# Two linear-attention and two segment-memory layers: one copy of 1024 columns per tile, opening stacks at once, and the last segment's output in column halves

## The chip, the cores and the metric

The kernel runs on one core of one Trainium2 chip. The metric is the device time of one execution in microseconds, as the median of several runs. Engines: PE multiplies matrices (PEld loads its weights), DVE, ACT and POOL work on vectors, and SP issues nearly all DMAs.

## The reference

A sequence of 2048 rows of 512 goes through four layers, each with layer normalisation ahead and a residual sum behind: A, B, A, B. Both have 32 heads of 16.

```python
def A(x):                                  # linear attention
    q, k, v = heads(x @ wqkv)
    pq, pk = q @ w_phi, k @ w_phi          # per head, 16 x 16
    phi_q = concat(softmax(pq), softmax(-pq)); phi_k = concat(softmax(pk), softmax(-pk))
    kv, z = phi_k.T @ v, phi_k.sum(rows)
    return (phi_q @ kv / (phi_q @ z)) @ wo

def B(x):                                  # 4 segments of 512 rows, with a memory M, z
    for s in range(4):
        p = softmax(causal(q[s] @ k[s].T / 4))
        a_mem = phi(q[s]) @ M / (phi(q[s]) @ z)
        o[s] = g * a_mem + (1 - g) * (p @ v[s])
        M, z = M + phi(k[s]).T @ v[s], z + phi(k[s]).sum(rows)
    return o @ wo
```

## The kernel before

Everything is in float32, products in pairs of high and low parts (`hh` and `hl`, `oh` and `ol`, `w` twice), so that one product is three matmuls per 128 rows of the contraction.

**Layer A** has two passes. The first makes keys, values and the sum kv, and stores the projected queries. The second, `pass2`, goes over 16 tiles of 128 rows. Per tile PE turns the tile before (`turn`, four transposes of `tmp` into one bank `g`), multiplies the tile's features with KN (32 small matmuls, which DVE weighs into `tmp`), turns the features of the tile to come (`transposed`, eight transposes into the PSUM tile `lg`, of two banks), and multiplies the output of the tile before with wo (`out_proj`, twelve matmuls). In the first tiles `transposed` stands behind `out_proj`, so the KN product of the same features follows it closely. ACT copies the turned features from PSUM to SBUF (`P`); POOL makes differences and scales them (`scale_q`); DVE sums the exponentials (`es`, `rr`).

**Layer B** is one loop over steps k, in `steps`. Four heads are a group m, five steps each (R = 5), eight groups to a segment, 32 groups in all. In each step `attend` makes scores into `lg`, ACT takes their exponential and POOL masks; `maxima` does the same scores into `mx`, `my` or `g` nine steps ahead (LEAD), for DVE to take their maxima. At the first step of a group PE also multiplies the probabilities of the group before with the values (`weighted`) and turns the result before that (`finish`). The tables FIRST, GAPS, and FINAL or LAST say what else each step does: `2.1 Q3/6` is six steps of the fourth projection in step 1 of group 2. Q, V, O and P are work for PE between the score steps: projections of queries and keys, values, the output of the segment before (`out`, `out_pair`), and the early part of the last output (`early`). LAST ends the first B layer, FINAL the second. `mm3_pair` lets two products of half the rows run side by side in the array; SP hands over between them.

**Stacks.** Scores need queries and keys as three stacked parts. `stack` issues three DMAs of them (`e<-ta`) on SP, for queries (side 0) and for keys (side 1), in steps 2 and 4 of a group (STACK), three groups ahead. The first two groups are stacked before step 0, in the opening, where second pass and layer B run into one another; there q0, v0, k0, v1, q1, k1 and v2 are projected first (BEFORE), and `queue_w` orders the next weights (`wqk`) behind each. SP takes its DMAs in order; one that waits holds those behind it.

Of the kernel before, what the change touches and what calls it, by code (L numbers as in the profile page):

```python
# [15 lines left out]
D = 512  # L16
# [67 lines left out]
"""  # L84
FINAL = """
0.0 a1 a1 max fin  | 0.1 Q2/6          | 0.2 Q2/6          | 0.3 Q2/6 | 0.4 Q2/6
1.0 max fin
2.0 turn max fin   | 2.1 Q3/6          | 2.2 Q3/6          | 2.3 Q3/6 | 2.4 Q3/6
3.0 turn a2 max fin | 3.1 O/6          | 3.2 O/6           | 3.3 O/6 | 3.4 O/6
4.0 turn a2 fin max  # L90
5.0 turn a3 a3 max fin  | 5.1 O/6           | 5.2 O/6           | 5.3 O/6 | 5.4 O/6
6.0 max fin        | 6.4 pre
7.0 pt pt fin max  | 7.1 P/4           | 7.2 P/5           | 7.3 P/5 | 7.4 P/4
"""
BEFORE = {-25: "q0 load", -23: "v0", -21: "k0",
          -18: "n", -17: "v1 n", -16: "n", -15: "n n", -14: "q1 n", -13: "n", -12: "k1 n", -11: "n", -10: "v2 n",
# [4 lines left out]
def interleave_kernel(ctx, tc, x_in, a_wqkv, a_wphi, a_wo, b_wq, b_wk, b_wv, b_wo, b_beta,  # L101
# [396 lines left out]
        wait(end)  # L498
        yield

    def out_pair(tiles, xdst, w):

        pos = [PS("g", G) for _ in tiles]

        def side(po, o):
            return po, lambda a, kc: o[a][:, kc * P : (kc + 1) * P], lambda b, kc: w[b][:, kc, :]

        yield from mm3_pair(*[side(po, o) for po, (x, i, o) in zip(pos, tiles)])

        def end():  # L510
            for po, (x, i, o) in zip(pos, tiles):
                y = T2("tb3", TB3)
                act.copy(y, po)
                pool.tensor_tensor(out=x, in0=y, in1=x, op=ADD)
                sync.dma_start(out=xdst[i], in_=x)
        wait(end)
        yield

    def weigh(out, p, eps, add, eng=pool):
# [123 lines left out]
    class LayerA:  # L643
# [268 lines left out]
        def pass2(self):  # L912

            KN = self.KN
            phT = {}

            def transposed(i):

                if i >= NT:
                    return
                ef = self.e.pop(i).rearrange("p h s f -> p (h s f)")
                phT[i] = T2("P4", NP4, shape=(P, 8, P))
                pt = PS("lg", 1, (P, 2, 512))
                for half in range(2):
                    for q in range(4):
                        g = 4 * half + q
                        tp(pt[:, half, q * P : (q + 1) * P], ef[:, g * P : (g + 1) * P], ident)
                    act.copy(phT[i][:, 4 * half : 4 * half + 4, :], pt[:, half].rearrange("p (g t) -> p g t", g=4))  # L930
                    yield

            yield from transposed(0)
            o = None
            for i in range(NT + 1):
                if i > 0:
                    oT = turn([o[:, c * P : (c + 1) * P] for c in range(NC)])
                    yield PAUSE if i == NT else None
                if i + 2 < NT:
                    exp(self.e[i + 2])  # L940
                if i < NT:
                    o = T2("tmp", 2)
                    f = phT.pop(i)
                    for half in range(2):
                        pn = PS("g", G)
                        pv = pn[:, 0 : 16 * VW].rearrange("p (g h e) -> p g h e", g=4, h=4)
                        for q in range(4):
                            g = 4 * half + q
                            for a in (0, 64):
                                mm(pn[a : a + 64, q * 4 * VW : (q + 1) * 4 * VW], lhsT=f[:, g, a : a + 64],  # L950
                                   rhs=KN[:, g].rearrange("p h e -> p (h e)"), start=True, stop=True,
                                   tile_position=(0, a))
                        weigh(o[:, half * 256 : half * 256 + 256].rearrange("p (g h d) -> p g h d", g=4, h=4),
                              pv, 0.0, False)
                        yield
                    if not 0 < i < 3:
                        yield from transposed(i + 1)
                    if i == 0:
                        self.begun(3)
                    if i + 3 < NT:  # L960
                        self.e[i + 3] = differences(*self.raw.pop(i + 3))
                    if i != 1 and i + 2 < NT:
                        scale_q(self.e[i + 2])
                    self.load_q(i + 4)
                    ahead = residual(self.xsrc, i, ("ot", OT))
                if i > 0:
                    yield from out_proj(x, self.xdst, i - 1, oT, self.wo)
                if 0 < i < 3:
                    yield from transposed(i + 1)
                if i == 1:  # L970
                    scale_q(self.e[i + 2])
                x = ahead


    class LayerB:
        def __init__(self, xsrc, xdst):
            self.xsrc, self.xdst = xsrc, xdst
            self.st, self.hT, self.vv, self.ot, self.mx, self.U = {}, {}, {}, {}, {}, {}
            self.pr, self.at, self.k, self.wo = {}, {}, BEGIN, []
            self.later, self.late, self.rows, self.turned = [], [], [], []  # L980

        def start(self):
# [262 lines left out]
        def out(self, s):  # L1245
            for t in (0, 2):
                tiles = [(x, 4 * s + t + n, oT) for n, (oT, x) in enumerate(self.turned[0:2])]
                del self.turned[0:2]
                yield from out_pair(tiles, self.xdst, self.wo)

        def early(self):

# [6 lines left out]
            for t in (0, 2):  # L1259
                o, po = [], []  # L1260
                for n in range(2):
                    o.append(turn([b[:, t + n] for b in ot]))
                    yield
                po = [PS("g", G) for _ in range(2)]

                def side(po, o):
                    return po, lambda a, kc: o[a][:, kc * P : (kc + 1) * P], lambda b, kc: self.wo[b][:, kc, :]

                if t == 0:
                    yield from mm3_pair(side(po[0], o[0]), side(po[1], o[1]), range(NC - 1))  # L1270
                else:
                    for n in range(2):
                        yield from mm3(*side(po[n], o[n]), range(NC - 1))

                def end(po=po, xs=self.xe[t : t + 2]):
                    for p, x in zip(po, xs):
                        dve.tensor_tensor(out=x, in0=p, in1=x, op=ADD)
                wait(end)
                yield
# [31 lines left out]
        def steps(self, side, after, table_end):  # L1311
# [81 lines left out]
            for k in range(BEGIN, R * N + 1):  # L1393
# [9 lines left out]
                for f in self.at.pop(k, []):  # L1403
                    f()
                m = k // R + 3
                if k % R in STACK and 0 <= m < N:
                    self.stack(m, STACK.index(k % R))
                if k == R * N:
                    for _ in range(4):
                        next(early)  # L1410
                if k % R == 0 and 0 <= k // R - 1 < N:
                    self.weighted(k // R - 1)
                for f in self.rows:
# [43 lines left out]
    run(p1[0], prepare())  # L1457
    for i in range(2):
        lb = LayerB(xs[2 * i + 1], xs[2 * i + 2])
        run(p1[i])  # L1460
        a2 = la[i].pass2()
        opening = lb.opening()
# [39 lines left out]
```

## Time and profile before

| | us |
|---|---|
| median of 3 runs (1478.45 to 1483.07) | 1481.69 |
| profiled execution | 1485.13 |
| its span, first to last instruction | 1483.4 |
| PE busy | 1385.0 |
| DVE busy | 1059.2 |
| ACT busy | 814.4 |
| POOL busy | 692.8 |
| mean granted PE clock | 0.986 |

Busy times overlap; they do not add up. A wait counts only where the waiting engine has nothing else and the end depends on it. In the timeline a row is start, duration, engine, line, operation, output and input, and in brackets the idle time before it and what ended it. The second passes lie at about 190 to 325 and 904 to 1046 us, the openings of layer B at 262 to 295 and 980 to 1010, and the last segment from 1366 to the end.

### The profile page before, as it was taken

Reading aid. Unit: us, or ns where it says so; the run is one execution under the profiler, and the core shown is the slowest. Engines: PE = TensorE matmul, PEld = TensorE weight load, DVE = VectorE, ACT = ScalarE, POOL = GpSimd, SP = SyncE. Lnnn points to the kernel's source line nnn. Section 1 sums busy time; section 2 is a strip of 40 time slices with the busy share of each in tenths; the row PEclk is TensorE's granted clock in tenths of the full one; section 3 lists DMA queues with packets and bytes.
Section 4 is the critical chain, followed back from the end, with each engine's and each line's share of the span. In section 5 each row is a group of like instructions: output and inputs, shape, how many; then the busy total and the mean of one; then the engine's idle time right before and its main releaser. Section 6 shows DMA issues by size and latency. Waiting matters only on the chain.

```text
span 1483.4 us, 33426 instructions
## 1 busy us (share of the span) xinstructions
PE 1385.0 (93%) x12412; PEld 1048.7 (71%) x12412; DVE 1059.2 (71%) x3258; ACT 814.4 (55%) x1226; POOL 692.8 (47%) x1024
## 2 busy tenths in 40 slices
PE   7999988899999999999999998898998999999887
PEld 6887867666676776777578887776666777777554
DVE  4666777477787787888656677746678878778772
ACT  5545345336566677576634434442556756766653
POOL 1568655304446547335324365532335556643341
PEclk9999999999999999999999999999999999999898
DMA  5387355435444444445431006643453453543431
GB/s 188 115 305 270 129 162 166 131 101 148 143 129 119 126 130 130 126 130 162 137 128 57 23 23 196 203 144 95 128 178 95 134 149 92 137 126 91 103 88 54
DMA packets 108786, 196.05 MB, mean 132 GB/s; under 512 B 14416, under 2 KB 27856, under 8 KB 107856
## 3 DMA queue, kind: packets, MB, share of 16 engines
q1 hardware_dynamic: 107472, 193.38, 43.8%
q8 instruction: 99, 1.62, 0.5%
q10 hardware_dynamic: 1152, 0.52, 0.1%
q14 instruction: 63, 0.52, 0.1%
HBM read 101.05 MB, written 39.85 MB: 95 GB/s over the span
## 4 chain that ended last, share of the span: by engine, by line
PE 71%; DVE 11%; ACT 7%; POOL 4%; issue 3%; DMA 3%; SPq 1%; ACTq 0%; DVEq 0%; POOLq 0%
PE g L178 53%; PE lg L178 6%; PE g L182 5%; ACT P L156 4%; PE mx L178 3%; PE lg L182 2%; PE my L178 1%; DVE es L156 1%; POOL P L156 1%; DVE g L156 1%; POOL tb L156 1%; SPq L156 1%; ACT U L156 1%; DVE my L156 1%; DVE mx L156 1%
## 5 line engine op out<-in xcount | busy, mean ns | idle before, releaser
L156 ACT ACTIVATE P<-lg 128x1024 f32<-128x1024 f32 x320 | 329.4, 1029 | 183.5 <-PE lg L178 103.1
L156 POOL TENSOR_SCALAR_AFFINE_SELECT P<-P 128x256 f32<-128x256 f32 (+1 forms) x448 | 193.6, 447 | 333.4 <-ACT P L156 333.1
L156 DVE CUSTOM_DVE_ANT_0 mx<-mx,mask 128x128 f32<-128x128 f32 (+3 forms) x332 | 165.1, 497 | 55.2 <-PE my L178 45.2
L156 DVE CUSTOM_DVE_ANT_0 g<-g,mask 128x512 f32<-128x512 f32 x360 | 175.8, 543 | 18.7 <-PE g L178 17.9
L178 PE MATMUL g<-hh,wqk 64*128 64x512 f32 (+1 forms) x960 | 184.9, 392 | 3.7 <-SPq L156 1.5
L178 PE MATMUL lg<-e,e 64*128 64x256 f32 (+2 forms) x1024 | 156.1, 359 | 23.1 <-ACT P L156 23.0
L178 PE MATMUL g<-w,oh 64*128 64x512 f32 (+1 forms) x728 | 169.4, 406 | 7.5 <-SPq L156 6.1
L156 DVE CUSTOM_DVE_ANT_0 my<-my,mask 128x128 f32<-128x128 f32 (+3 forms) x332 | 172.2, 519 | 0.0
L178 PE MATMUL g<-P,v 128*32 128x512 f32 (+3 forms) x2048 | 156.1, 446 | 4.6 <-DVE mxs L156 4.3
L178 PEld LDWEIGHTS lg<-e,e 64*128 64x128 f32 x1024 | 93.8, 189 | 74.2 <-ACT P L156 50.0
L178 PE MATMUL g<-w,hh 64*128 64x512 f32 (+2 forms) x800 | 145.4, 357 | 0.6 <-DVE ol L156 0.6
L156 DVE DVE_READ_ACCUMULATOR2_ANT mxs<- 128x1 f32 x1024 | 143.7, 140 | 0.0
L178 PEld LDWEIGHTS g<-P,v 128*32 128x32 f32 x2048 | 61.0, 112 | 93.3 <-issue 67.7
L156 POOL TENSOR_SCALAR tb<-tb 128x512 f32<-128x512 f32 x72 | 110.9, 1552 | 27.2 <-ACT tb L156 27.2
L178 PEld LDWEIGHTS g<-hh,wqk 64*128 64x128 f32 (+1 forms) x960 | 104.2, 185 | 20.6 <-SPq L156 2.0
L178 PEld LDWEIGHTS g<-w,oh 64*128 64x128 f32 (+1 forms) x728 | 93.7, 190 | 28.2 <-SPq L156 8.7
L178 PE MATMUL g<-hl,wqk 64*128 64x512 f32 (+1 forms) x480 | 106.1, 390 | 0.5 <-DVE hl L156 0.5
L156 ACT COPY tb<-g 128x512 f32<-128x512 f32 x144 | 80.4, 588 | 46.7 <-PE g L178 44.8
L178 PE MATMUL g<-w,ol 64*128 64x512 f32 (+1 forms) x364 | 104.0, 400 | 0.4 <-DVE ol L156 0.4
L178 PEld LDWEIGHTS g<-w,hh 64*128 64x128 f32 (+1 forms) x800 | 92.0, 187 | 13.4 <-DVE ol L156 1.0
L178 PE MATMUL mx<-e,e 63*128 63x256 f32 (+2 forms) x332 | 89.7, 334 | 7.6 <-DMA e<-ta 7.6
L156 DVE TENSOR_TENSOR ol<-g,oh 128x512 fp32r<-128x512 f32 (+1 forms) x66 | 43.6, 673 | 74.5 <-ACT oh L156 74.5
(148 smaller groups left out, 2983.1 us busy)
## 6 DMA issues: line engine op xcount, KB each, us to landing
e<-ta SPq DMA_DIRECT2D x384, 128.0 KB
wqk<-wqk SPq DMA_DIRECT2D x64, 512.0 KB
x<-x SPq DMA_DIRECT2D x48, 256.0 KB
ot<-in SPq DMA_DIRECT2D x28, 256.0 KB
pq<-tb SPq DMA_DIRECT2D x24, 256.0 KB
tb<-pq SPq DMA_DIRECT2D x24, 256.0 KB
x<-xr SPq DMA_DIRECT2D x22, 256.0 KB
xr<-x SPq DMA_DIRECT2D x20, 256.0 KB
```

The lines of the kernel that those rows point to most:

```text
L156: i = f(*a, **k)
L178: return held(nc.tensor.matmul(*a, **k))
L182: return held(nc.tensor.transpose(*a))
```

## The change

It has three parts.

1. `transposed` copies the two halves of `lg` in one instruction of 1024 columns, behind the eighth transpose.
2. The first two groups are stacked, queries and keys, at the first slot of their group of steps (steps -15 and -10).
3. In FINAL the work is dealt anew. Of the last segment's groups 0 to 7, group 1 gets the projection Q3 that stood in group 2; the output of the segment before, which stood in groups 3 and 5, goes in halves of 256 columns over groups 2 to 5 (`thin`); the early output's first half goes from group 7 to 6 and its second half from the end to group 7. Turning two tiles at a time (`turn turn`) and the memory reads (`a2 a2`, `a3 a3`) move accordingly. In `early` the second half is now done by `mm3_pair` too, in both B layers.

```diff
-2.0 turn max fin   | 2.1 Q3/6          | 2.2 Q3/6          | 2.3 Q3/6 | 2.4 Q3/6
...
-4.0 turn a2 fin max
...
+1.0 turn turn max fin | 1.1 Q3/6       | 1.2 Q3/6          | 1.3 Q3/6 | 1.4 Q3/6
...
+4.0 turn turn fin max | 4.1 O/6        | 4.2 O/6           | 4.3 O/6 | 4.4 O/6
...
-    def out_pair(tiles, xdst, w):
+    def out_pair(tiles, xdst, w, w0=0, w1=D):
...
-            return po, lambda a, kc: o[a][:, kc * P : (kc + 1) * P], lambda b, kc: w[b][:, kc, :]
+            return (po[:, 0 : w1 - w0], lambda a, kc: o[a][:, kc * P : (kc + 1) * P],
+                    lambda b, kc: w[b][:, kc, w0:w1])
...
+        for po, (x, i, o) in zip(pos, tiles):
+            y = T2("tb3", TB3)[:, 0 : w1 - w0]
+            act.copy(y, po[:, 0 : w1 - w0])
+            pool.tensor_tensor(out=x[:, w0:w1], in0=y, in1=x[:, w0:w1], op=ADD)
+            if w1 == D:
                 sync.dma_start(out=xdst[i], in_=x)
...
-                    act.copy(phT[i][:, 4 * half : 4 * half + 4, :], pt[:, half].rearrange("p (g t) -> p g t", g=4))
+                    if half == 1:
+                        act.copy(phT[i].rearrange("p g t -> p (g t)"), pt.rearrange("p h x -> p (h x)"))
...
-                yield from out_pair(tiles, self.xdst, self.wo)
+                parts = 2 if self.thin and s == NSEG - 2 else 1
+                for n in range(parts):
+                    yield from out_pair(tiles, self.xdst, self.wo, n * D // parts, (n + 1) * D // parts)
...
-                if t == 0:
-                    yield from mm3_pair(side(po[0], o[0]), side(po[1], o[1]), range(NC - 1))
-                else:
-                    for n in range(2):
-                        yield from mm3(*side(po[n], o[n]), range(NC - 1))
+                yield from mm3_pair(side(po[0], o[0]), side(po[1], o[1]), range(NC - 1))
...
-                if k % R in STACK and 0 <= m < N:
-                    self.stack(m, STACK.index(k % R))
+                if 0 <= m < N:
+                    for side_ in range(2):
+                        if k % R == (STACK[side_] if m > 1 else 0):
+                            self.stack(m, side_)
                 if k == R * N:
                     for _ in range(4):
-                        next(early)
+                        next(early, None)
```

On ACT, in the second pass (P is the SBUF copy or the features, lg the PSUM tile, oh the high part of the turned output), before:

```order
L156 CAST oh_2346<-g_2348 128x512
L156 ACTIVATE P_388_2316<-P_388_2316 128x1024
L156 COPY P_402_2381<-lg_2382 128x512 x2
L156 CAST oh_2421<-g_2423 128x512
L156 ACTIVATE P_404_2393<-P_404_2393 128x1024
```

and after:

```order
L156 CAST oh_2341<-g_2343 128x512
L156 ACTIVATE P_388_2311<-P_388_2311 128x1024
L156 COPY P_402_2376<-lg_2377 128x1024
L156 CAST oh_2415<-g_2417 128x512
L156 ACTIVATE P_404_2387<-P_404_2387 128x1024
```

Two copies have become one; nothing changes place.

On SP, in the first opening (e is a stack, ta the high or low part of a projection, wqk weights, x the second pass's output on its way to memory), before:

```order
L156 DMA wqk_3071<-wqk_82 128x1024
L156 DMA wqk_3126<-wqk_81 128x1024
L156 DMA e_432_2495<-ta_544_3026 32x2x512 x2
L156 DMA e_432_2495<-ta_545_3027 32x2x512
L156 DMA wqk_3157<-wqk_82 128x1024
L156 DMA e_433_2496<-ta_556_3073 32x2x512
L156 DMA e_433_2496<-ta_557_3074 32x2x512
L156 DMA e_433_2496<-ta_556_3073 32x2x512
L156 DMA x_10_93<-ot_2906 128x512
```

and after:

```order
L156 DMA wqk_3058<-wqk_82 128x1024
L156 DMA e_432_2488<-ta_544_3013 32x2x512 x2
L156 DMA e_432_2488<-ta_545_3014 32x2x512
L156 DMA e_433_2489<-ta_556_3060 32x2x512
L156 DMA e_433_2489<-ta_557_3061 32x2x512
L156 DMA e_433_2489<-ta_556_3060 32x2x512
L156 DMA wqk_3119<-wqk_81 128x1024
L156 DMA wqk_3147<-wqk_82 128x1024
L156 DMA e_432_2488<-ta_544_3013 32x2x512 x2
```

The first group's six stack DMAs now stand ahead of the two weight loads, and the second group's right behind these.

On PE, in steps 1 and 2 of group 4 of the last segment (lg: scores, mx, my and the `g` of e and e: scores for the maxima), before:

```order
L178 MATMUL lg_18969<-e_2273_12060,e_2274_12061 128x512 x2
L178 MATMUL mx_18976<-e_2293_12143,e_2292_12142 128x256
L178 MATMUL my_18977<-e_2293_12143,e_2292_12142 128x256
L178 MATMUL mx_18976<-e_2293_12143,e_2292_12142 128x384
L178 MATMUL my_18977<-e_2293_12143,e_2292_12142 128x384
L178 MATMUL lg_18986<-e_2273_12060,e_2274_12061 128x256 x2
L178 MATMUL lg_18986<-e_2273_12060,e_2274_12061 128x384 x2
```

and after, from the last maxima of step 1 on:

```order
L178 MATMUL my_19034<-e_2293_12139,e_2292_12138 128x384
L178 MATMUL g_19043<-w_13651,oh_18989 128x256
L178 MATMUL g_19044<-w_13651,oh_19000 128x256
L178 MATMUL g_19043<-w_13652,oh_18989 128x256
L178 MATMUL g_19044<-w_13652,oh_19000 128x256
L178 MATMUL g_19043<-w_13651,ol_18990 128x256
L178 MATMUL g_19044<-w_13651,ol_19001 128x256
L178 MATMUL g_19043<-w_13651,oh_18989 128x256
L178 MATMUL g_19044<-w_13651,oh_19000 128x256
L178 MATMUL g_19043<-w_13652,oh_18989 128x256
L178 MATMUL g_19044<-w_13652,oh_19000 128x256
L178 MATMUL g_19043<-w_13651,ol_18990 128x256
```

Before, the scores of a step follow the maxima of the step before at once; now six pairs of the output, 256 columns wide, lie between them.

More of the change, by code (lines that the diff above doesn't have):

```diff
@@ L86 @@
 0.0 a1 a1 max fin  | 0.1 Q2/6          | 0.2 Q2/6          | 0.3 Q2/6 | 0.4 Q2/6
-1.0 max fin
-2.0 turn max fin   | 2.1 Q3/6          | 2.2 Q3/6          | 2.3 Q3/6 | 2.4 Q3/6
-3.0 turn a2 max fin | 3.1 O/6          | 3.2 O/6           | 3.3 O/6 | 3.4 O/6
-4.0 turn a2 fin max
-5.0 turn a3 a3 max fin  | 5.1 O/6           | 5.2 O/6           | 5.3 O/6 | 5.4 O/6
-6.0 max fin        | 6.4 pre
-7.0 pt pt fin max  | 7.1 P/4           | 7.2 P/5           | 7.3 P/5 | 7.4 P/4
+1.0 turn turn max fin | 1.1 Q3/6       | 1.2 Q3/6          | 1.3 Q3/6 | 1.4 Q3/6
+2.0 max fin        | 2.1 O/6           | 2.2 O/6           | 2.3 O/6 | 2.4 O/6
+3.0 a2 a2 max fin  | 3.1 O/6           | 3.2 O/6           | 3.3 O/6 | 3.4 O/6
+4.0 turn turn fin max | 4.1 O/6        | 4.2 O/6           | 4.3 O/6 | 4.4 O/6
+5.0 a3 a3 max fin  | 5.1 O/6           | 5.2 O/6           | 5.3 O/6 | 5.4 O/6
+6.0 max fin pre    | 6.1 pt pt         | 6.2 P/6           | 6.3 P/6 | 6.4 P/6
+7.0 pt pt max fin  | 7.1 P/4           | 7.2 P/5           | 7.3 P/5 | 7.4 P/4
 """
@@ L499, in out_proj @@
         yield
-    def out_pair(tiles, xdst, w):
+    def out_pair(tiles, xdst, w, w0=0, w1=D):
         pos = [PS("g", G) for _ in tiles]
         def side(po, o):
-            return po, lambda a, kc: o[a][:, kc * P : (kc + 1) * P], lambda b, kc: w[b][:, kc, :]
+            return (po[:, 0 : w1 - w0], lambda a, kc: o[a][:, kc * P : (kc + 1) * P],
+                    lambda b, kc: w[b][:, kc, w0:w1])
         yield from mm3_pair(*[side(po, o) for po, (x, i, o) in zip(pos, tiles)])
[L510 to L514, printed above, removed]
+        for po, (x, i, o) in zip(pos, tiles):
[3 more added lines that the diff above has]
+            if w1 == D:
                 sync.dma_start(out=xdst[i], in_=x)
-        wait(end)
         yield
@@ L978, in __init__ @@
             self.st, self.hT, self.vv, self.ot, self.mx, self.U = {}, {}, {}, {}, {}, {}
-            self.pr, self.at, self.k, self.wo = {}, {}, BEGIN, []
+            self.pr, self.at, self.k, self.wo, self.thin = {}, {}, BEGIN, [], False
             self.later, self.late, self.rows, self.turned = [], [], [], []
@@ L1459, in interleave_kernel @@
         lb = LayerB(xs[2 * i + 1], xs[2 * i + 2])
+        lb.thin = i == 1
         run(p1[i])
```

## Prediction

> **What bounds the kernel.** I read the page first, for the engine that the end hangs on, then the waits of that engine, then the timeline at each place the change touches, then one row per block of the last segment.
>
> ```profile
> PE 1385.0 (93%) x12412; PEld 1048.7 (71%) x12412; DVE 1059.2 (71%) x3258; ACT 814.4 (55%) x1226; POOL 692.8 (47%) x1024
> PE 71%; DVE 11%; ACT 7%; POOL 4%; issue 3%; DMA 3%; SPq 1%; ACTq 0%; DVEq 0%; POOLq 0%
> ...
> PE lg L182 <- ACT P L156: 23.3, 32, 1.1
> PE lg L178 <- ACT P L156: 23.0, 53, 1.3
> ...
> PE mx L178 <- DMA e<-ta: 7.6, 2, 4.2
> ```
>
> PE is busy 93% of the span and 71% of the chain that ended last, so a saving must be a saving of PE time. The three waits (total us, times, longest) belong to the three parts of the change: 32 waits of the transposes of the second linear pass (16 tiles, two passes) on the copy; the waits of score matmuls on the exponential, most of all where no projection lies between them, as in parts of the last segment; and two waits on the opening stacks, one in each B layer.
>
> **Part 1, one copy of 1024 columns.** PE in one tile of the second pass, and POOL and DVE beside it:
>
> ```profile
> 940.97 0.60 PE L182 MATMUL g<-ident,tmp 128*128 128x128 f32 x4
> 942.60 0.66 PE L182 MATMUL lg<-ident,P 128*128 128x128 f32 x4
> 943.93 0.66 PE L182 MATMUL lg<-ident,P 128*128 128x128 f32 x4 [0.68 <-ACT P L156]
> 944.34 0.71 PE L178 MATMUL g<-w,oh 128*128 128x512 f32 x2
> ...
> 946.84 1.06 POOL L156 TENSOR_TENSOR P<-P,rr 128x512 f32<-128x512 f32 x1 [1.86 <-DVE rr L156]
> 947.21 0.60 PE L182 MATMUL g<-ident,tmp 128*128 128x128 f32 x4
> 948.83 0.66 PE L182 MATMUL lg<-ident,P 128*128 128x128 f32 x4
> ```
>
> The second four transposes start 1.33 us after the first four and wait for the copy of the first half. Four take 0.41 (943.93 to 944.34). In the batch the second four follow at once: 1.33 - 0.41 = 0.92 us of PE time less. Nothing else in the tile makes PE wait, so a tile falls from 6.24 us (940.97 to 947.21) to about 5.3. The copy loses its overlap and is read later, but the matmuls that read it stand in the next tile, more than 4 us on.
>
> That holds for tiles 4 to 15. In tiles 0 to 3 the matmuls with KN follow the transposes at once:
>
> ```profile
> 920.45 0.60 PE L182 MATMUL lg<-ident,P 128*128 128x128 f32 x4
> ...
> 922.80 1.17 PE L178 MATMUL g<-KN,P 128*64 128x68 f32 x32
> ...
> L156 ACT ACTIVATE P<-lg 128x1024 f32<-128x1024 f32 x320 | 329.4, 1029 | 183.5 <-PE lg L178 103.1
> ```
>
> Today 2.35 us lie between them. The new copy is not in the trace; its bounds are nothing above one old copy (0.59 us, the second in the old order) and two of them (1.18). The nearest row is the exponential of the same PSUM tile and size, 1.03. Transposes 0.41 + 0.66, copy 1.03, some 0.1 of semaphores: 2.2. So these eight tiles gain 0.1 each or lose as much, and I take 0. Part 1: 24 x 0.92 = 22.1.
>
> What is late next: POOL's multiplication of the following tile ends at 947.90 and its transposes start at 948.83, 0.93 later. With tiles 0.92 shorter that slack is gone in the tiles where DVE also does layer statistics, as here. I take off 0.5 us per pass (bounds 0 and the whole 0.92 in half of the tiles, 5.5).
>
> A rule against this part stands in the Trainium skill, PSUM — Partial Sum Buffer, Summary: rules for kernel authors: to read PSUM while matmuls run, aim at a different bank. The two halves are two banks of 512 FP32 each, so by it halves could overlap and the batch would give the overlap away. The trace disagrees for this program: the second half waited all the same (0.68 us, above). By that rule alone part 1 would be worth 0 and not 22.
>
> **Part 2, opening stacks.** PE, then DVE and SP's queue before it, then PE in the first layer, and the stretch behind each stall (columns: length, PE, PEld, DVE, ACT, POOL, clock, DMA share, GB/s):
>
> ```profile
> 1003.54 0.55 PE L178 MATMUL mx<-e,e 63*128 63x256 f32 x1 [3.42 <-DMA e<-ta]
> 1004.37 1.22 PE L178 MATMUL g<-w,oh 128*128 128x512 f32 x2
> ...
> 990.55 0.69 DVE L156 TENSOR_TENSOR ta<-tb,ta 128x512 fp32r<-128x512 f32 x1 [4.75 <-ACT ta L156]
> 989.27 5.76 SPq L156 DMA_DIRECT2D wqk<-wqk  x2
> 995.13 1.86 SPq L156 DMA_DIRECT2D e<-ta  x3
> 997.86 2.05 SPq L156 DMA_DIRECT2D e<-ta  x3
> ...
> 285.61 0.35 PE L178 MATMUL mx<-e,e 63*128 63x256 f32 x1 [4.18 <-DMA e<-ta]
> ...
> 286.00:289.00 3.00, 3.00 (x9) 2.10 (x8) 1.64 (x8) 0.00 (x0) 3.00 (x3) 0.50 0.00 0
> 1003.50:1009.00 5.50, 5.46 (x30) 4.14 (x30) 2.52 (x10) 0.81 (x2) 4.29 (x4) 0.50 0.02 8
> ```
>
> The last part that a stack copies is ready at 991.24 (DVE), but its DMAs stand behind the second of two weight loads, which waits for PE till about 994.7 (995.03 less its own issue); the stack is issued by 999.91 and lands at 1003.5, 3.6 us later. Moved ahead of that load, six DMAs of about 0.6 us start at 989.6, wait for 991.24, and end by about 993.5; with the same 3.6 they land at 997.1. PE gets there at about 1000.1 (1003.54 less its wait). The stall goes whole: 3.4 + 4.2 = 7.6. The two loads behind wait for PE as they do now, and the second stack's six DMAs follow them with the time of a whole head group. Stores to x, now behind these, are awaited by nobody here.
>
> After the stall the granted clock is 0.50. In 5.5 us, half of the PE time is the excess: 2.7; in the first layer 3.0 us: 1.5. Both go with the stall. Part 2: 7.6 + 4.2 = 11.8. In the 40 us behind it DVE is the busiest after PE, and without stall and half clock it is nearly full; I take off 1 us a layer (bounds 0 and 2).
>
> **Part 3, the last segment.** One row for each of the head groups 1 to 6 (score step to score step, columns as above), and last a group of the second segment, where halves of 256 columns already fill every step:
>
> ```profile
> 1378.54:1393.06 14.52, 11.28 (x75) 5.75 (x74) 9.95 (x38) 7.99 (x11) 5.13 (x9) 0.65 0.36 94
> 1393.06:1405.26 12.20, 12.20 (x126) 9.21 (x126) 9.06 (x36) 7.58 (x11) 3.68 (x8) 1.00 0.37 88
> 1405.26:1417.89 12.63, 12.34 (x126) 9.36 (x126) 11.86 (x42) 8.81 (x12) 8.39 (x11) 1.00 0.38 101
> 1417.89:1432.88 14.99, 10.76 (x83) 5.99 (x82) 10.52 (x42) 6.82 (x9) 3.67 (x8) 0.77 0.35 92
> 1432.88:1445.00 12.12, 11.52 (x119) 8.38 (x118) 9.09 (x38) 6.95 (x9) 6.16 (x10) 1.00 0.07 26
> 1445.00:1458.83 13.83, 9.12 (x59) 4.35 (x58) 0.92 (x3) 6.44 (x8) 3.71 (x8) 0.63 0.27 95
> ...
> 1087.07:1098.74 11.67, 9.86 (x118) 6.83 (x117) 8.01 (x33) 6.77 (x10) 3.82 (x9) 1.00 0.56 159
> ```
>
> Groups 1, 4 and 6 have no projection between the score steps. They are the longest: PE waits for the exponential, and its clock falls to 0.63 to 0.77. The change fills all of them. Splitting columns adds no PE time: three pairs of 256 take 0.35, half of three pairs of 512.
>
> ```profile
> 1075.22 0.40 PE L178 MATMUL g<-w,hh 64*128 64x256 f32 x4
> 1075.46 0.28 PE L178 MATMUL g<-w,hl 64*128 64x256 f32 x2
> ...
> 1405.90 0.64 PE L178 MATMUL g<-w,oh 64*128 64x512 f32 x4
> 1406.37 0.41 PE L178 MATMUL g<-w,ol 64*128 64x512 f32 x2
> ```
>
> (Two pairs, then the third: 0.24 and 0.47 to the third.) New: group 0 gets eight transposes behind it (0.82, partly in PE's wait for U), +0.5; 1 has the projection, 12.1; 2 to 5 half filled, 11.67 as the row of the second segment, to which turning or memory reads add 0.1 to 0.4 that partly lie in PE's wait for U: 11.8, 11.9, 11.8, 11.6; 6 has the last output's first half and no maxima, 11.5. Sum 71.2, against 80.3 now: 9.1. Bounds: 12.6 for every half-filled group (the fullest row at full clock), 5.7 in all; 11.4 for each, 10.5.
>
> At the end PE now turns and multiplies the last output's second half: six matmuls ahead of the last values, twelve behind them while DVE weighs:
>
> ```profile
> 1465.44 0.44 PE L182 MATMUL g<-ident,ot 128*128 128x128 f32 x2
> ...
> 1468.48 2.36 PE L178 MATMUL g<-P,v 128*32 128x512 f32 x32
> 1471.65 0.66 PE L182 MATMUL g<-ident,U 128*128 128x128 f32 x4 [0.81 <-ACT U L156]
> ...
> 1472.31 2.78 PE g L178 x12
> ...
> 1473.17 0.42 DVE L156 TENSOR_TENSOR tmp<-tmp,wt 128x256 f32<-128x256 f32 x1
> ```
>
> They move into group 7 as pairs. The turning and the six come off, 1465.4 to 1468.5: 3.0. The weighing ends at 1473.6, 1.3 behind the transposes of U, and the twelve matmuls that cover it take 2.8: 1.3 more, with the semaphores. But then PE idles 0.8 us for U, 1.4 for the weighing and some 0.7 for the last split, and gaps of that kind brought the clock down in groups 1, 4 and 6. At half clock those and their transposes cost 1.5 more. Part 3: 9.1 + 4.3 - 1.5 = 11.9.
>
> The Trainium skill, TensorE: Matmul & The Clock Gate, HAM oscillation — how this bites in real kernels, says that PE gaps above some 3.4 us drop the clock. By that rule the end would keep its clock and the sum be 1.5 larger. The trace does not agree: the clock fell in group 4 with no wait above 1.3 us (the longest in the row of waits).
>
> Moved at no cost: in the first B layer the output's second half becomes pairs too, 18 x 0.23 either way. The residual loads go a group earlier.
>
> **Sum.** 22.1 - 1 + 11.8 - 2 + 11.9 = 42.8. The profiled execution took 1485.1 (span 1483.4), so 1442.3 there; the runs' median, 1481.7, is 3.4 lower, so 1439; I say 1440.
>
> **Rivals.** (a) DVE and POOL become the bound in pass 2. For it: the 0.93 of slack. Against: DVE is 71% busy over the span, and lags heal in tiles without statistics. Some 14 us lost: 1454. (b) Half-filled groups let the clock fall. For it: group 4. Against: the row of 1087.07, clock 1.00. With 9 lost, 1449. (c) The end keeps its clock (the rule above): 1438. (d) The batch does not save what it says, because the wait hid something that ends as late: 1440 + 22 = 1462; against it, no other PE wait stands in a tile. (e) Slower: a fuller PE is granted a lower clock everywhere. Mean now 0.986; PE carries nearly all of the span, so a fall by 2.9%, to 0.957, eats the 42 us, and one by 4%, to 0.947, ends at 1440 x 1.04 = 1498. Against it: from 1393.06 to 1405.26 PE is busy for 12.20 of 12.20 at 1.00.
>
> **Numbers.** Forecast 0.58, a 0.12, b 0.10, c 0.12, d 0.04, e 0.04. Range 1430 (no friction, groups of 11.4, the clock kept at the end: 48.7 off, and 3 for a new copy near its lower bound in the eight early tiles) to 1456 (past a and b); outside lie d, e and a part of a. Less than 0.3% (4.4 us) cannot be told from no change: faster 0.96; of e, slower 0.03 and same 0.01.
>
> **What would show it.** Step 1: no wait of second-pass transposes on ACT, tiles of 5.3 us; if they stay above 5.8, a or d, and the waits name DVE or POOL. Step 2: no wait on the stacks, clock 1.00 behind v's projection. Step 3: no group above 12.7, clock 1.00 in all of them; from the last values' start to the end 15.1 us, or 13.6 if the clock holds, against 14.9 now (1468.48 to 1483.4). A clock mean below 0.98 makes me wrong by e.

## The result and the profile after

The kernel after took 1444.15 us, the median of four runs (1442.99 to 1444.48), against 1482.38 before (four runs); the ratio is 0.9743, 95% interval 0.9719 to 0.9766. The forecast was 1440, its range 1430 to 1456. The profiled execution took 1442.99 us (span 1441.3), 42.1 less than that of before. In a second comparison it took 1442.32 (1441.87 to 1443.05), with a ratio of 0.9732 (0.9710 to 0.9754).

The page after, its lines on the engines:

```profile
PE 1372.0 (95%) x12544; PEld 1049.0 (73%) x12544; DVE 1057.3 (73%) x3258; ACT 808.9 (56%) x1198; POOL 691.5 (48%) x1028
```

PE lost 13.0 us of busy time, most of it matmuls at half clock (before, the clock was at 0.50 for 41 us inside the work, after for 7); the other 29 us were idle. The waits of PE after (total us, times, longest):

```profile
PE lg L178 <- ACT P L156: 14.3, 56, 0.6
PE g L182 <- DMA P<-in: 9.6, 1, 9.6
PE g L178 <- ACT P L156: 6.6, 8, 1.1
...
PE g L182 <- DVE tmp L156: 1.3, 1, 1.3
```

The 23.3 us of second-pass transposes on ACT and the 7.6 on the stacks are gone, the scores wait 14.3 and not 23.0. New are 6.6 us in eight places: in tiles 0 to 3 the matmuls with KN wait for the large copy. Transposes of two tiles that follow each other, and the group of the new copies (us in total, mean ns), priced at 1.03:

```profile
906.54 1.09 PE L182 MATMUL lg<-ident,P 128*128 128x128 f32 x8
...
911.90 1.09 PE L182 MATMUL lg<-ident,P 128*128 128x128 f32 x8
...
L156 ACT COPY P<-lg 128x1024 f32<-128x1024 f32 x32 | 32.4, 1014 | 33.9 <-PE lg L182 31.2 <-issue 2.7
```

A tile takes 5.36, the copy 1.014. The last segment, one row for each head group 0 to 6, then group 7 up to the last values, then from these to the end (columns: length, PE, PEld, DVE, ACT, POOL, clock, DMA share, GB/s):

```profile
1334.05:1346.21 12.16, 12.16 (x126) 9.12 (x125) 9.13 (x39) 7.54 (x10) 3.67 (x8) 1.00 0.52 132
1346.21:1359.44 13.23, 11.92 (x118) 9.36 (x118) 10.96 (x39) 8.83 (x14) 5.29 (x9) 1.00 0.43 122
1359.44:1371.12 11.68, 10.72 (x127) 7.92 (x127) 10.62 (x41) 8.15 (x12) 6.92 (x11) 1.00 0.31 69
1371.12:1382.49 11.37, 10.55 (x126) 7.64 (x125) 9.12 (x39) 7.10 (x10) 5.01 (x10) 1.00 0.51 137
1382.49:1394.39 11.90, 10.98 (x127) 7.96 (x126) 9.98 (x40) 6.99 (x11) 5.00 (x10) 1.00 0.37 95
1394.39:1405.66 11.27, 9.85 (x119) 6.81 (x119) 8.81 (x38) 6.51 (x9) 5.01 (x10) 1.00 0.19 64
1405.66:1418.55 12.89, 11.80 (x103) 7.10 (x102) 3.23 (x7) 7.32 (x10) 3.69 (x8) 1.00 0.22 71
1418.55:1425.15 6.60, 6.42 (x51) 4.23 (x51) 1.37 (x4) 3.63 (x5) 2.62 (x6) 1.00 0.01 2
1425.15:1441.30 16.15, 9.43 (x54) 5.78 (x52) 5.85 (x10) 1.85 (x3) 0.64 (x1) 0.76 0.17 65
```

The clock is 1.00 in every group and falls only at the end. With landmarks taken from the two timelines, the 42.1 us divide like this (both layers together where there are two):

| stretch | before | after | difference | forecast |
|---|---|---|---|---|
| start to the second pass, first layer | 185.33 | 183.19 | -2.1 | - |
| second pass to v0, the opening's first projection of values | 79.62 + 79.66 | 71.85 + 72.06 | -15.4 | -15.6 |
| from there to the first maxima (stalls) | 20.66 + 19.90 | 16.41 + 16.41 | -7.7 | -7.6 |
| first maxima to v's last projection (half clock, tiles 13, 14) | 21.47 + 22.59 | 19.86 + 19.86 | -4.3 | -5.9 |
| from there to the first scores (tile 15) | 12.48 + 12.50 | 11.58 + 11.60 | -1.8 | -1.8 |
| head groups between, outside the last segment | 584.42 + 327.84 | 583.90 + 327.33 | -1.0 | - |
| last segment to its last values | 102.01 | 91.10 | -10.9 | -12.1 |
| last values to the end | 14.92 | 16.15 | +1.2 | +0.2 |

So 3.1 us of the 42.1 lie where the forecast had nothing. Of the 2.1 in the first row, 0.6 is PE's wait for the first inputs (10.2 and 9.6 us) and 0.6 its waits for POOL (2.3 and 1.7); the rest is spread over the first pass. This row and that of the head groups scatter whatever the kernel: over the fourteen profiled executions of this study the second pass began anywhere from 181.95 to 188.54 us, and the head groups of the first B layer took 582.32 to 587.62.

### The profile page after: what moved, and what is told of

It is laid out like the page before. It is cut to its first block, busy times and chain, and to the rows that moved or that the text cites. A ratio compares the mean times of both kernels' runs of the same rounds, so it can differ in the third digit from the quotient of the medians.

```text
span 1441.3 us, 33697 instructions
## 1 busy us (share of the span) xinstructions
PE 1372.0 (95%) x12544; PEld 1049.0 (73%) x12544; DVE 1057.3 (73%) x3258; ACT 808.9 (56%) x1198; POOL 691.5 (48%) x1028
## 4 chain that ended last, share of the span: by engine, by line
PE 69%; DVE 12%; ACT 7%; POOL 5%; issue 3%; DMA 2%; SPq 1%; ACTq 0%; DVEq 0%; POOLq 0%
PE g L178 52%; PE lg L178 6%; PE g L182 5%; PE mx L178 3%; ACT P L156 3%; DVE es L156 2%; POOL tb L156 2%; POOL P L156 2%; PE lg L182 1%; PE my L178 1%; DVE g L156 1%; ACT U L156 1%; DMA wqk<-wqk 1%; DVE my L156 1%; DVE mx L156 1%
## 5 line engine op out<-in xcount | busy, mean ns | idle before, releaser
L178 PE MATMUL g<-hh,wqk 64*128 64x512 f32 (+1 forms) x960 | 188.1, 392 | 3.5 <-DMA wqk<-wqk 2.0
L156 DVE CUSTOM_DVE_ANT_0 g<-g,mask 128x512 f32<-128x512 f32 x360 | 175.9, 543 | 15.2 <-PE g L178 14.4
L178 PE MATMUL g<-w,oh 64*128 64x512 f32 (+2 forms) x816 | 172.2, 385 | 6.8 <-SPq L156 5.0
L178 PE MATMUL lg<-e,e 64*128 64x256 f32 (+2 forms) x1024 | 154.5, 353 | 14.5 <-ACT P L156 14.3
L178 PE MATMUL g<-P,v 128*32 128x512 f32 (+3 forms) x2048 | 151.1, 435 | 4.3 <-DVE mxs L156 4.0
L178 PEld LDWEIGHTS g<-hh,wqk 64*128 64x128 f32 (+1 forms) x960 | 108.2, 185 | 20.0 <-ACT hh L156 1.8
L178 PEld LDWEIGHTS g<-w,oh 64*128 64x128 f32 (+1 forms) x816 | 98.2, 188 | 28.9 <-SPq L156 9.6
L178 PE MATMUL g<-w,ol 64*128 64x512 f32 (+2 forms) x408 | 106.8, 379 | 1.0 <-DVE ol L156 1.0
L156 ACT COPY tb<-g 128x512 f32<-128x512 f32 (+1 forms) x148 | 80.9, 576 | 45.5 <-PE g L178 43.6
L178 PE MATMUL g<-w,hl 64*128 64x512 f32 (+2 forms) x400 | 93.7, 355 | 0.0
```

The costliest lines, as they stand in the source:

```text
L156: i = f(*a, **k)
L178: return held(nc.tensor.matmul(*a, **k))
```

## The experiments

**Each part by itself, and part 3 from the other side.** The edit of the first is the hunk of `transposed` alone, of the second that of `steps` alone (the condition on STACK), of the third all others; the fourth has the first two.

> The kernel before with part 1 alone: one ACT copy of 1024 columns for a tile's transposed features; stacks and the last segment's table as before. Theory (each part pays by itself, part 1 by some 0.85 us in each of the tiles 4 to 15 of two passes, as the trace of after shows: 45.14 us where before had 51.85 for eight tiles): 1482 - 20 = 1462, within 1459 to 1465; the waits on the stacks stay at 7 to 8 us. Rival (the gain of pass 2 was only possible because the stacks had gone, or is taken back by a longer wait for them, whose DMAs hang on weight loads): 1470 or more, with waits of the maxima on the stack's DMA above 12 us.

> The kernel before with part 2 alone: the stacks of the two opening half groups at the first slot. Theory (stall 7.6 and half clock behind it 4.2, friction at most 2): 1482 - 10 = 1472, within 1470 to 1474, no wait of the maxima on e<-ta, clock 1.00 in all of the stretch behind the first maxima. Rival (the stall is the only cost, the clock falls there anyway because v's projection follows the turned tiles): 1475, with the clock still at 0.50 in the 3 to 5 us behind.

> The kernel before with part 3 alone: the last segment's table, column halves of the output projection, the last output's pairs. Theory (after's trace: from the first score step of the last segment to the last values 91.1 us against 102.0 before, and from these to the end 16.2 against 14.9): 1482 - 10 = 1472, within 1469.5 to 1474.5. Rival (the segment is faster only because work of the passes before it reached it earlier): same, 1478 or more.

> The kernel before with parts 1 and 2, without part 3: the old table of the last segment, no column halves, the old last output. What part 3 is worth is then read from the other side. Theory (part 3 is worth the 9.7 us of the traces, and its 5.1 when it was tried alone came out small by scatter): 1443 + 9.7 = 1453, within 1450.5 to 1456. Rival (it is worth some 5, because part of what its groups save comes back as waits elsewhere): 1446 to 1449.5. By sums of single edits, 1482 - 19.3 - 11.2 = 1451.

| kernel | median us (runs) | ratio to before, 95% | less than before's median |
|---|---|---|---|
| copy only | 1462.24 (1459.6 to 1463.2) | 0.9858 (0.9826 to 0.9891) | 19.3 |
| stacks only | 1470.38 (1467.76 to 1474.75) | 0.9919 (0.9888 to 0.9950) | 11.2 |
| last segment only | 1476.46 (1474.79 to 1481.01, ten runs) | 0.9968 (0.9953 to 0.9982) | 5.1 |
| copy and stacks | 1451.77 (1449.58 to 1454.32) | 0.9794 (0.9769 to 0.9818) | 29.6 |

Parts 1 and 2 pay by themselves, within their bounds, and add up (19.3 + 11.2 = 30.5, together 29.6). With the copy alone the waits on the stacks stay at their size:

```profile
PE mx L178 <- DMA e<-ta: 7.7, 2, 3.9
```

Part 3 alone missed its bounds: 5.1 us, where its own trace shows the last segment up to its last values at 91.65 us and the end at 16.17, against 102.01 and 14.92: 9.1 less. That holds in every profile: with the old table (before, copy only, stacks only, copy and stacks, idle work in the stalls) the segment and its end take 116.9 to 117.6 us together, with the new one (last segment only, after, two banks) 107.2 to 107.8. Taken out of the kernel after, part 3 is worth 1451.77 - 1442.3, 9.5 (7.6 against the 1444.15 of the first comparison; these are medians of different comparisons). The rival, that the groups' gain comes back elsewhere, is not borne out by that; why the ten runs alone lie some 4 us higher than the trace says stays open.

**Idle work in the stalls.** Part 2 was priced as a stall and a half clock behind it. Here the stall stays and only the idleness goes:

```diff
+                if m == 0 and what[0] == (0, 0, 0):
+                    pw = PS("mx", 1)
+                    for a in range(30):
+                        tp(pw[:, a % 4 * P : (a % 4 + 1) * P], ident, ident)
```

> The kernel before with idle work for TensorE in the two stalls on the opening stacks: 30 transposes of the identity (0.107 us each, 3.2 us) ahead of the first maxima of each B layer, where PE waits 4.2 and 3.4 us for the stack's DMA; their results are not read. The stalls stay, TensorE is only kept busy in them. Theory (part 2 took away the stalls, 7.6, and the half clock behind them, priced at 4.2 from one profile; the second alone is taken away here): the clock stays 1.00 behind both, the stretch from the first maxima to v's third projection falls from 21.5 and 22.6 us to about 20, and the time by the mean price of the half clock: 4.2 as priced, less if not every execution pays it (of the five profiled stalls of this kind two had full clock or nearly so behind them): 1477.5 to 1480 against 1481.5. Rival (the clock falls with the transfer or with v's projection, and not with the idle TensorE): 0.50 there still, 1481 or more.

It took 1476.8 us against 1481.48, ratio 0.9972 (0.9957 to 0.9986): 4.7 us, with bounds of 2.1 and 6.4, and 0.7 below the range expected. PE in the first layer's stall, which the idle transposes fill but for 0.95 us, and v's projection behind it, at 0.73 for two where before had 1.22:

```profile
277.92 3.44 PE L182 MATMUL mx<-ident 128*128 128x128 f32 x30
282.31 0.35 PE L178 MATMUL mx<-e,e 63*128 63x256 f32 x1 [0.95 <-DMA e<-ta]
...
282.80 0.73 PE L178 MATMUL g<-w,oh 128*128 128x512 f32 x2
```

From the first maxima to v's last projection 19.92 and 19.93 us, where before had 21.47 and 22.59. The half clock is caused by the idle TensorE, and in the profile of before it cost 1.55 + 2.66 = 4.2.

**Two banks in place of a batch.**

```diff
-                pt = PS("lg", 1, (P, 2, 512))
+                two = i <= 12
+                pts = [PS("mx", 1), PS("my", 1)] if two else PS("lg", 1, (P, 2, 512))
...
+                    if two:
+                        act.copy(phT[i][:, 4 * half : 4 * half + 4, :], pt.rearrange("p (g t) -> p g t", g=4))
```

> The kernel after, but the tiles 0 to 12 of the second pass put each half of the transposes into a PSUM tile of its own (mx and my, a bank each) and copy each half by itself, as 512 columns, as before; tiles 13 to 15 stay batched. Theory (the wait of before was one of the program: both halves lay in one tile of two banks, so the second half's transposes were made to wait for the copy that reads the first; with tiles of their own they need not wait): no wait of these transposes on ACT, tiles of 5.3 us, and in tiles 0 to 3 some 0.3 us each less since the first half's copy runs early; in all 1440 to 1445. Rival (ACT reading one bank while TensorE writes the next holds one of them up, or two copies cost ACT the time that batching saved): the transposes of 0.66 us get longer or the tiles 0.4 us or more longer, 1452 to 1462.

1443.26 us (1443.0 to 1446.01), ratio 0.9737 (0.9711 to 0.9764): as after. PE in tile 4:

```profile
201.46 0.66 PE L182 MATMUL mx<-ident,P 128*128 128x128 f32 x4
201.96 0.60 PE L182 MATMUL my<-ident,P 128*128 128x128 f32 x4
...
206.82 0.66 PE L182 MATMUL mx<-ident,P 128*128 128x128 f32 x4
```

The second half starts 0.50 behind the first, without a wait, while ACT copies the first; tiles again take 5.36. The wait of before was the program's: in this kernel two halves in one tile were ordered as one thing, and with a tile for each the wait is gone. The Trainium skill, PSUM — Partial Sum Buffer, Summary: rules for kernel authors, advises another bank for reading PSUM while matmuls run; this trace agrees with it, and what the rule could not see is that here two banks of one tile did not count as two. Tiles 0 to 3 gain besides: 183.12 to 201.46 is 18.34, where after takes 19.76 (183.19 to 202.95).

**Whole columns.** The output projection in pairs of 512, three a step, where after has pairs of 256, six a step.

```diff
-2.0 max fin        | 2.1 O/6           | 2.2 O/6           | 2.3 O/6 | 2.4 O/6
+2.0 max fin        | 2.1 O/3           | 2.2 O/3           | 2.3 O/3 | 2.4 O/3
...
-        lb.thin = i == 1
+        lb.thin = False
```

(The same in the rows 3 to 5.)

> The kernel after once more, unchanged, beside the three others of this call: 1444 within 1442.5 to 1446 on this chip too.

> The kernel after with the output projection of the last segment in whole columns (pairs of 512) at three pairs a step, where it has column halves (pairs of 256) at six pairs a step; the same steps of the table are filled with the same PE time. Theory (filling the empty groups is the gain, the halves only make the grain finer): same as after, 1442.5 to 1445.5, groups 2 to 5 at 11.3 to 12.0 and the clock at 1.00. Rival (the halves matter, because a whole pair is evicted in copies of 512 columns that delay the exponential on ACT, or because it holds its PSUM tiles longer): groups 2 to 5 together 1.5 us or more longer, 1446 to 1450.

The kernel after took 1442.32, just under its bounds, whole columns in the same comparison 1445.5 (1444.31 to 1445.83, and one run of 1454.89): 3.2 us more, with runs that do not overlap. The time lies at the upper edge of the theory and 0.5 under the rival's, but the groups decide for the rival: groups 2 to 5 take 48.95 us, 2.7 more than in after. Groups 2, 4 and 6, where after has 11.68, 11.90 and 12.89 (this is the run of 1454.89, which also began its second pass at 188.54):

```profile
1367.65:1380.70 13.05, 11.34 (x103) 6.90 (x102) 11.29 (x43) 7.61 (x10) 5.13 (x9) 1.00 0.27 62
...
1392.06:1405.34 13.28, 11.38 (x104) 6.95 (x103) 10.80 (x42) 6.45 (x9) 3.66 (x8) 1.00 0.39 106
...
1416.60:1430.44 13.84, 12.76 (x102) 8.22 (x102) 3.33 (x7) 7.41 (x10) 3.70 (x8) 0.88 0.26 85
```

Groups 3 and 5 did not change (11.36 and 11.26). PE's waits in group 4 that after does not have there:

```profile
PE g L182 <- ACT mt L156: 0.4, 1, 0.4
PE g L182 <- DVE r L156: 0.2, 1, 0.2
```

They stand before the transposes at the group's end. ACT's `mt` (the turned maxima) and DVE's `r` (reciprocals of sums) read tiles of `g`: the transposes of U (the weighted values) start when `mt` is done, at 1404.75, though U was ready at 1403.12, so they wait for a PSUM tile. These two waits are 0.6 of the 1.4 us; PE is also busy 0.4 longer (11.38 and 10.98), and the scores wait 0.3 longer for the exponential (1.2 and 0.9), so the rival's other half, the larger copies on ACT, may have a small share. A pair of column halves takes 24 steps, one group, and its two PSUM tiles of `g` (of four) are free when the group ends. A whole pair lasts two groups; at the end of groups 2 and 4 it still holds two of the four, while the values, two memory reads and two sets of transposes take turns at the rest. The experiment on the turning, below, shows the same by another edit.

**Idle work at the end.**

```diff
+            heat(6)
             self.finish(N - 1)
...
+            heat(10)
             o = self.end_turn()
...
+            heat(5)
             self.end(o)
```

`heat(n)` is n transposes of the identity into `mx`, in the last layer.

> The kernel after with idle work for TensorE in the three waits of its end: 6 transposes of the identity behind the last values, 10 behind the transposes of U, 5 behind the last turning, 0.1 us each, so that they fit into the waits of 0.81, 1.34 and 0.68 us; their results are not read. Theory (short waits that follow each other bring the granted clock down, a TensorE kept busy keeps it): clock 1.00 up to the last matmul, the twelve last matmuls in 2.8 us and not 5.3, the last turning in 0.66 and not 1.12, so 1444 - 2.9 = 1441. Rival 1 (the clock falls at the end for another reason, for instance because transposes do not count as work): 0.50 there still, 1444. Rival 2 (the idle work is in the way of what waits behind it): above 1445.

1440.97 us (1440.16 to 1441.35), 1.35 below after in the same comparison, with no overlap of the runs; ratio to before 0.9722 (0.9700 to 0.9743). From the last values' start to the end:

```profile
1425.77:1439.50 13.73, 9.44 (x75) 6.10 (x73) 5.85 (x10) 1.86 (x3) 0.64 (x1) 1.00 0.20 77
```

The clock stays, and the stretch takes 13.73 where the profiles of after have 16.15 and 15.2 (1426.1 to 1441.3). The mechanism is right and the size was too large: 2.9 expected, 1.35 found by the medians, 1.5 to 2.4 by the profiles.

**Real work at the end, with and without two other edits.** The edit of the end, common to the three:

```diff
-7.0 pt pt max fin  | 7.1 P/4           | 7.2 P/5           | 7.3 P/5 | 7.4 P/4
+7.0 pt pt max fin  | 7.1 P/2           | 7.2 P/3           | 7.3 P/3 | 7.4 P/2
...
                     self.weighted(k // R - 1)
+                if k == R * N and self.thin:
+                    for _ in range(3):
+                        next(early, None)
```

and in the first of them the turning and the output projection:

```diff
-4.0 turn turn fin max | 4.1 O/6        | 4.2 O/6           | 4.3 O/6 | 4.4 O/6
-5.0 a3 a3 max fin  | 5.1 O/6           | 5.2 O/6           | 5.3 O/6 | 5.4 O/6
-6.0 max fin pre    | 6.1 pt pt         | 6.2 P/6           | 6.3 P/6 | 6.4 P/6
+4.0 turn turn fin max | 4.1 O/5        | 4.2 O/6           | 4.3 O/5 | 4.4 O/5
+5.0 a3 a3 max fin  | 5.1 O/5           | 5.2 O/5           | 5.3 O/6 | 5.4 O/5
+6.0 max fin pre    | 6.1 O/6           | 6.2 pt pt P/5     | 6.3 P/6 | 6.4 P/7
```

> The kernel after with two places of the last segment mended. First, eight of the last output's 18 pairs of steps (0.23 us each) leave group 7: three stand behind the last values, where PE waits 0.81 us for U, five behind the transposes of U, where it waits 1.34 us for the weighing. Second, the turning in group 6 moves from its second step, where PE waits 0.89 us for POOL and the clock then falls, to its third; the output projection of the segment before is dealt to one more step. Theory (work in the waits is free and keeps the clock): 1.8 from the pairs, 2.5 to 2.9 from the clock at the end, 0.9 and some 0.7 in group 6: 1444 - 6 = 1438, between 1437 and 1440. Rival (the pairs pass SP's queue at their change of rows and their additions on DVE stand before the last split, so that what is won ahead of the last values is lost behind them): 1442 or more.

> The kernel after with the second of these two changes alone: eight pairs of the last output behind the last values. Theory (work in the waits, and a clock that does not fall): 1.9 us less than after, 1440.4, within 1439.2 to 1441.5, with clock 1.00 to the last matmul and 13.8 us from the last values' start to the end. Rival (only the clock counts, the moved work is won ahead of the values and lost behind them): as with the idle work, 1441 with 14.4 us or more from the last values' start.

> The kernel after with two changes. First, a PSUM tile of its own for each half of the transposes in tiles 0 to 12 of the second pass, each half copied by itself, as tried above. Second, eight of the last output's 18 pairs of steps moved from group 7 into the two waits behind the last values, as tried above, the turning of group 6 left as it is in after. Theory (the traces: tiles 0 to 3 take 18.34 us where the batch takes 19.76, in two passes 2.8; from the start of group 7 to the end 19.9 where after has 21.8 to 22.75, 1.9 at least): 1442.3 - 4.7 = 1438, within 1436 to 1440. Rival (the 1.4 us of a pass come back as a longer wait behind it, as the two banks showed only 0.9 us less than after in their median): 1440.5 or more.

With the turning moved: 1443.96 (1441.4 to 1445.65), no gain, where 1438 was expected. Its groups 4 and 6 and its end:

```profile
1384.23:1397.49 13.26, 11.66 (x120) 7.76 (x119) 10.80 (x42) 6.45 (x9) 3.66 (x8) 1.00 0.32 85
...
1408.76:1422.81 14.05, 12.64 (x115) 7.82 (x114) 3.24 (x7) 7.75 (x12) 5.03 (x10) 1.00 0.11 40
...
1428.88:1442.70 13.82, 9.21 (x70) 5.07 (x68) 5.85 (x10) 2.29 (x3) 0.63 (x1) 1.00 0.20 78
```

The end has 13.82, as hoped, but group 4 takes 1.36 more and group 6 1.16 more than in after. Group 6 had full clock in after too, so the expected gain of 0.7 from its clock was not there to be had; in its new place the turning stands right ahead of the first pairs, and PE waits 0.7 us for ACT's `oh` and 0.5 for an exponential. In group 4 the last half pair is three steps short at the group's end and keeps its two PSUM tiles; the memory reads, first of after and then of this kernel, show it:

```profile
1392.72 1.19 PE L178 MATMUL g<-mem,tb 128*128 128x136 f32 x8
...
1394.45 1.61 PE L178 MATMUL g<-mem,tb 128*128 128x136 f32 x8
```

The end alone: 1440.73 (1438.2 to 1445.59, six runs; 1440.4 expected), ratio 0.9728 (0.9703 to 0.9753), from the last values' start to the end 13.9 us; of the three waits only the last is left:

```profile
1427.96 0.63 PE L182 MATMUL g<-ident,tmp 128*128 128x128 f32 x4
1429.27 0.73 PE L178 MATMUL g<-w,oh 128*128 128x512 f32 x2 [0.68 <-ACT oh L156]
```

The end with two banks: 1441.8 (1438.92 to 1442.25; 1438 expected, and the rival's 1440.5 or more came), ratio 0.9718 (0.9695 to 0.9742). Its second passes are 1.4 and 0.9 us shorter than after's up to v0 (70.47 and 71.18), which its time does not show; it also began the first of them at 184.79, 1.6 later than after. Between the last two kernels and after, each in its own comparison, the medians differ by 1.6 and 0.5 us while their runs overlap: neither is shown to be faster. Only the idle work is, by 1.35 us.

## Why the prediction was right, and where its terms were off

**Step 1, the batch.** Tiles of 5.36 (forecast 5.3), the waits on ACT gone, and the friction where it was looked for. POOL in one of these tiles and the transposes behind it:

```profile
229.06 1.06 POOL L156 TENSOR_TENSOR P<-P,rr 128x512 f32<-128x512 f32 x1 [2.32 <-DVE rr L156]
...
230.18 1.09 PE L182 MATMUL lg<-ident,P 128*128 128x128 f32 x8 [0.39 <-POOL P L156]
```

In the second row of the table above the forecast (nine tiles of 0.92 less 0.5, twice) stands at 15.6, measured 15.4. That they meet so closely is luck. In two tiles of each pass of before the wait on the copy was not 0.68 but 0.9 and 1.13:

```profile
244.66 0.66 PE L182 MATMUL lg<-ident,P 128*128 128x128 f32 x4 [1.13 <-ACT P L156]
```

So 0.65 a pass more could be gained than was forecast, and tiles 0 to 3 gained 0.17 where 0 was taken; against that the friction was 1.3 and 1.5 a pass and not 0.5. The term was too large for tiles 13 and 14, which lie in the opening of the B layer: with the stacks alone (old copies, no stall, clock 1.00) that stretch took 20.18 and 20.19, in after 19.86 twice. Two batches of 0.92 less the friction of 1 should have been worth 0.84 a layer and are worth 0.3. The row there, and PE's waits in it:

```profile
271.45:291.31 19.86, 18.50 (x176) 13.67 (x175) 18.60 (x62) 9.11 (x14) 8.38 (x7) 1.00 0.31 94
...
PE g L182 <- DVE xr L156: 0.6, 1, 0.6
PE my L178 <- DVE mxs L156: 0.3, 2, 0.2
PE mx L178 <- DVE mxs L156: 0.2, 1, 0.2
```

DVE is busy for 18.60 of 19.86 us, more than PE. The 1.4 us for which PE waits there for the copies with the stacks alone are gone, and in their place it waits 1.1 us for DVE (`xr` is the residual sum, `mxs` the maxima). The friction was named ("nearly full") and set in the middle of its bounds, 1 a layer; it was 1.5, in the upper half. That is rival (a) in the one place where DVE is full, not over the pass.

**Step 2, the stacks.** Stall 7.7 (forecast 7.6), no wait on the stacks left, clock 1.00. The half clock, priced at 4.2, is 4.2 by the run in which it alone is taken away and 3.7 by the one with the stacks alone (20.18 + 20.19 against 21.47 + 22.59).

**Step 3, the last segment.** Its groups saved 8.0 in groups 1 to 6 (80.3 to 72.34) and lost 0.1 in group 0: 7.9, where 9.1 was forecast. Five groups came out at or below their forecast, but for 0.1 in group 4. Two did not: group 1, 13.23 for 12.1 (14.16 in after's second profile), in which PE waits 0.7 us for weights and 0.6 for U, in the second profile 1.6 and 0.6, so that the 0.9 between the two is the weights; no experiment took these waits away, and the same projection in group 2 of before had none; and group 6, 12.89 for 11.5, whose turning waits 0.89 us for the weighing on POOL. Behind it, at a clock of 1.00, the weight loads (PEld) of the first pairs wait for ACT, DVE and SP, 1.0 us in all, and the pairs are slow until that is over:

```profile
1407.41 0.33 PE L182 MATMUL g<-ident,tmp 128*128 128x128 f32 x1 [0.89 <-POOL tmp L156]
...
1408.40 1.02 PE L178 MATMUL g<-w,oh 64*128 64x512 f32 x4
1408.69 0.29 PEld L178 LDWEIGHTS g<-w,oh 64*128 64x128 f32 x3 [0.20 <-ACT oh L156]
...
1409.36 0.18 PEld L178 LDWEIGHTS g<-w,ol 64*128 64x128 f32 x1 [0.28 <-DVE ol L156]
...
1410.17 0.30 PEld L178 LDWEIGHTS g<-w,oh 64*128 64x128 f32 x4 [0.52 <-SPq L156]
...
1411.26 0.62 PE L178 MATMUL g<-w,oh 64*128 64x512 f32 x4
```

Thus step 3's "no group above 12.7" failed twice. The term of group 6 was mis-sized: its 11.5 had nothing for the wait of its turning or for the weight loads behind it. The wait for POOL had no row in before. The end saved 3.05 ahead of the last values (forecast 3.0) and lost 1.2 behind them (forecast 0.2): the half clock there cost not 1.5 but up to 2.4, since it also lasts through nearly all of the last split's twelve matmuls.

```profile
1430.31 1.12 PE L182 MATMUL g<-ident,tmp 128*128 128x128 f32 x4 [1.34 <-DVE tmp L156]
1432.11 1.22 PE L178 MATMUL g<-w,oh 128*128 128x512 f32 x2 [0.68 <-ACT oh L156]
```

Rival (c), that the end keeps its clock, fell, and with it the rule of the Trainium skill that stood behind it: TensorE: Matmul & The Clock Gate, HAM oscillation — how this bites in real kernels, speaks of gaps above some 3.4 us, and here the longest is 1.34. Rival (b) fell too: half-filled groups with waits of 0.2 to 0.3 us a step keep 1.00. The price of column halves at nothing stood on the PE time of a pair and said nothing of how long a pair holds PSUM; in whole columns the same filling would have been worth 3.2 less.

**The sum.** Parts 1 and 2 were to give 30.9 in the profile and gave 29.2, part 3 11.9 and gave 9.7. The forecast from the profile, 1442.3, came within 0.7 us of the profiled execution because 3.1 us of start and scatter, which nobody forecast, filled most of the gap: the mechanisms were right, the closeness of the sum was luck. By the medians the change is worth 38.2 and 39.4 in the two comparisons; 42.8 was 3 to 5 too much.

## What to carry to other kernels

A stall of TensorE can be dearer than its length, since half clock may follow it: price both, and put any independent work, even useless work, into short waits that follow one another. A wait between halves of a buffer may belong to the buffer and not to the hardware; a tile for each half removes it as well as a batch does. Where work is dealt into gaps, cut it so that a piece ends where its PSUM is needed by others, and look at the busiest other engine of each stretch, not of the span, before a saving of PE time is counted there.

## What the runs showed of the hardware

- The granted clock changed only at points 3.41 us apart. In the clock record of the fourteen profiled executions it is 1.00 or 0.50, and half clock lasts 3.41, 6.83 or 10.24 us wherever the execution goes on behind it. What went with a change was how much of the step of 3.41 us before it PE was busy: after 44% or less the clock fell each time (26 of its 41 falls), after 60% or more never, between the two sometimes; it came back after 88% or more and stayed at half after 80% or less. One row for each step around the two stalls of before, then around the first stall with the last segment only (columns as above):

```profile
282.50:285.91 3.41, 0.30 (x4) 0.33 (x4) 0.00 (x0) 2.13 (x4) 3.00 (x3) 1.00 0.38 133
285.91:289.33 3.42, 3.42 (x12) 2.43 (x9) 1.79 (x9) 0.00 (x0) 3.25 (x3) 0.50 0.00 0
...
999.30:1002.71 3.41, 0.82 (x4) 0.36 (x2) 0.69 (x1) 3.38 (x7) 1.19 (x1) 1.00 0.76 254
1002.71:1006.12 3.41, 2.58 (x8) 1.99 (x9) 1.64 (x8) 0.62 (x1) 3.33 (x4) 0.50 0.01 3
1006.12:1009.54 3.42, 3.42 (x25) 2.49 (x24) 1.43 (x3) 1.35 (x2) 1.75 (x2) 0.50 0.19 72
...
277.63:281.04 3.41, 1.59 (x8) 0.97 (x6) 0.69 (x1) 3.38 (x6) 0.44 (x1) 1.00 0.94 296
281.04:284.46 3.42, 1.77 (x10) 1.40 (x11) 1.21 (x7) 1.37 (x3) 3.34 (x3) 1.00 0.05 17
```

- One stall has no fixed price. With a stall of 3.4 to 4.2 us ahead, the stretch from the first maxima to v's last projection took 21.47 and 22.59 us in before, 21.53 and 20.74 with the copy only, 19.92 and 22.43 with the last segment only, and 19.92 and 19.93 with TensorE kept busy: once nothing was lost, at the most 2.7. The stall of 3.46 us that cost nothing lay across two steps (the last two rows) and left PE busy for about half of each; one of 3.42 (before, second layer) lay mostly in one step and was followed by 6.83 us of half clock. That the place of a stall in the steps sets its price fits the rows here, but no run moved a stall to try it.
- At the end of after the clock fell behind waits of 0.81 and 1.34 us, at 1430.2, in one profile, and behind these and one of 0.68, at 1433.4, in the other; PE was busy for 40% and 44% of the step before. With work in the first two waits the third alone did not lower it, and transposes of the identity, 0.107 us each, were enough to hold it.
- Runs of before spread over 1476 to 1489 in the last comparison (17 runs), those of after over 1441.9 to 1444.5 in both of its own (eight runs). That fewer stalls, each with an uncertain price, leave less to vary is likely from the point above, and was not tried by itself.
